# First expert search with masks in halves, bank-held thresholds and a new order of its neighbours

## The chip, the cores and the metric

The kernel runs on one core of a Trainium2 chip. The metric is the device time of one execution in microseconds; the time of a kernel is the median of its runs. The core's engines are TensorE (PE; the loading of its weights is shown apart as PEld), VectorE (DVE), ScalarE (ACT), GpSimd (POOL) and SyncE (SP), each with a queue of its own that it works through in order. Transfers are issued by SP and POOL and carried by 16 DMA engines.

## The reference

A local and summary attention gives 1536 tokens of 512 numbers. They go through a mixture of 8 experts of exactly 192 tokens each, then through a dense layer pair (`_moe2_ref`). What matters here is how tokens come to experts: all 12288 logits are walked from the largest down, and a token goes to an expert that still has room.

```python
def _moe_ref(x, w_gate, w1, w2):
    N, D = x.shape
    E = w_gate.shape[1]
    cap = N // E
    order = np.argsort(-(x @ w_gate).flatten())
    assigned = -np.ones(N, dtype=np.int64)
    counts = np.zeros(E, dtype=np.int64)
    for idx in order:
        tok, e = int(idx) // E, int(idx) % E
        if assigned[tok] >= 0 or counts[e] >= cap:
            continue
        assigned[tok] = e
        counts[e] += 1
    ...
    for e in range(E):
        mask = assigned == e
        out[mask] = np.maximum(x[mask] @ w1[e], 0.0) @ w2[e]
    return out

def _moe2_ref(x, w_in, w_out):
    h = x @ w_in
    g = np.where(h >= 1, h, np.where(h <= -1, 0.0, (h + 1) ** 2 / 4))
    return g @ w_out
```

## The kernel before

**The search.** The greedy walk is done in eight phases, one for each expert that fills up. `Router.phase(k)` (line 554) works on 128 partitions by `NT` = 12 token columns. The token's best open expert is `oh` (one-hot). A threshold is found in `LEVELS` = 5 rounds of `KARY` = 32 steps: VectorE makes a mask `mk` of every token against 32 levels (line 713, in `pairwise`); twelve small matmuls (line 601) count the tokens over each level for each expert; VectorE subtracts the room that is left, reduces, and makes flags `fl`; one matmul (line 611) adds the flags up to the next offset `c`, in PSUM. After the last round the members: `vz` is the distance to the threshold, `cm` compares it with -0.5 and +0.5 of the last step, `X` holds who is assigned. A matmul (line 624) and a reduction `nn` (line 641) count per expert, two matmuls (line 635) and an ACT copy `tot` (line 638) give the totals ahead of every column, `f`, `fm`, `es` choose the expert that is full, `ei` is its number (SP reads it, to address the weights), `pos` and `slot` give every token its place, and `S` is a one-hot of places in two halves (line 713 again). `place` (line 722) multiplies it with `num`, the token numbers; the result, copied by ACT to `idx`, is a list of 192 tokens. The first phase runs alone; each later one runs beside the products of the expert before.

**The experts.** `fetch(k)` (line 759) gathers the 192 rows by POOL in two indirect DMAs of 96 rows; for `k == 0` SP also stores 32 bytes of the second half away, so SP waits there for that half. `weights(k, j)` issues four transfers of 1 MB for expert `k` from SP as soon as its number is known (stage "expert") and a slot is free. `transposed(k, h)` (line 797) turns one half of the tokens with four PE transposes, and ACT copies it to `xt`. `mlp(k)` is 64 steps: 32 first-layer products (line 816) and 32 second-layer ones (line 825). PE handles one such float32 product as two passes, each shown as one instruction of 192 columns; so "x6" of the trace are three products.

**What sets the order.** `run_experts` writes both threads into PE's queue. For each stage the search yields, one number of `PLAN` is taken. For the first `WAIT` stages after the first list was placed, and before that, the number is a count of blank matmuls (line 745, on a tile of zeros); the two stages named in `HALVES` also turn a half of the first expert's tokens. After that the number is a count of products. The tokens of expert `k + 1` are turned in `products()` at step 48 of `mlp(k)`, if they are placed by then. VectorE's conversions for the dense layers are also handed out here, one every `PACE` stages.

Of the kernel before, what the change touches and what calls it, by code (L numbers as in the profile page):

```python
# [8 lines left out]
F32 = mybir.dt.float32  # L9
# [24 lines left out]
RAWS = 9  # L34

PLAN = """
3 2 3 2 1 2 2 2 2 2 2 2 2 2 1 10 12 3 2 2 2 3 3 3 3 3 2 2 9 9 2 3 3 3 3 3 3 3 3 2 2 16 9 3 3 3 3 3 3 3 3 3 2 2 10
12 2 3 3 3 3 3 3 3 3 2 2 10 9 3 4 3 3 4 3 3 3 3 2 2 10 9 2 3 3 3 4 3 3 3 3 2 2 10 6 8 10
"""

WAIT = 5
HALVES = 3, 4

PACE = 4
TAIL = 2
# [368 lines left out]
class Router:  # L414
# [19 lines left out]
    def consts(self):  # L434
# [18 lines left out]
            g.tensor_scalar(self.lev[j], ki[:, :KARY], float(KARY) ** -j, None, op0=OP.mult)  # L453
            g.memset(self.unit[j], float(KARY) ** -j)
        self.rev = st.tile([128, E], BF, name="rev")
        self.num = st.tile([128, E], F32, name="num")
        g.tensor_scalar(self.rev, ki[:, :E], -1.0, E + 1.0, op0=OP.mult, op1=OP.add)
        g.tensor_scalar(self.num, ki[:, :E], -1.0, None, op0=OP.add)
        self.tok = st.tile([128, NT], HF, name="tok")
        t = st.tile([128, NT], F32, name="tokf")  # L460
        g.iota(t, pattern=[[128, NT]], base=0, channel_multiplier=1, allow_small_or_imprecise_dtypes=True)
# [92 lines left out]
    def phase(self, k):  # L554
# [13 lines left out]
        if not last:  # L568
            oh = self.oh
            for j in range(LEVELS):  # L570
# [9 lines left out]
                                                   c[:, :, None].to_broadcast([128, NT, 2]), op0=OP.subtract,  # L580
                                                   op1=OP.subtract)
                mk = wk.tile([128, NT, KARY], BF, name="mk")
                self.pairwise(mk, zi, self.lev[j], OP.is_ge)
                if k and j == 0:
                    self.close()
                if j < LEVELS - 1:
# [21 lines left out]
                nc.vector.tensor_scalar(fl, fm.to_broadcast([KARY, 2]), 0.0, None, op0=OP.is_ge)  # L608
                yield "flags"
                p = self.ps()  # L610
                nc.tensor.matmul(p[:, :2], self.unit[j][:KARY], fl, start=True, stop=True)
                c = p[:, 0:1].to_broadcast([128, NT])
            v = wk.tile([128, NT], F32, name="vz")
            nc.vector.tensor_tensor(v, zi[:, :, 0], c, op=OP.subtract)

            cm = wk.tile([128, 2] + full[1:], BF, name="cm")
            vb = v[:, :, None].to_broadcast(full)
            for i in range(2):
                nc.vector.scalar_tensor_tensor(cm[:, i], vb, (i - 0.5) * u, oh, op0=OP.is_ge, op1=OP.mult)
            nc.vector.tensor_tensor(X[:, 0], self.asg, cm[:, 1], op=OP.add)  # L620
            nc.vector.tensor_tensor(X[:, 1], cm[:, 0], cm[:, 1], op=OP.subtract)
            yield "members"
            pn = self.ps()
            nc.tensor.matmul(pn[:, :2 * NT * E], self.unit[0], cm.rearrange("p i t e -> p (i t e)"),
                             start=True, stop=True)
        else:

            self.close()
            nc.vector.tensor_copy(X[:, 0], self.asg)
            nc.vector.tensor_scalar(X[:, 1], v[:, :, None].to_broadcast(full), 0.0, None, op0=OP.is_ge)  # L630
            yield "members"

        pt = self.ps()
        for i in range(2):
            nc.tensor.matmul(pt[:NT * E, i * 128:(i + 1) * 128], X[:, i].rearrange("p t e -> p (t e)"), self.unit[0],
                             start=(i == 0), stop=(i == 1), skip_group_check=True)
        tot = wk.tile([NT * E, 2, 128], BF, name="tot")
        nc.scalar.activation(tot.rearrange("p i q -> p (i q)"), pt[:NT * E, :256], AF.Copy)
        if not last:
            nn = wk.tile([128, 2, E], F32, name="nn")  # L640
            nc.vector.tensor_reduce(nn, pn[:, :2 * NT * E].rearrange("p (i t e) -> p i e t", i=2, e=E),
                                    axis=AX.X, op=OP.add)
            nc.vector.tensor_tensor(f, nn[:, 0], self.left, op=OP.is_ge)
        else:
            nc.vector.tensor_scalar(f, self.left, CAP + 0.5, None, op0=OP.is_lt)
# [3 lines left out]
                                       op0=OP.mult, op1=OP.max, accum_out=fm)  # L649
        es = wk.tile([128, E], BF, name="es")  # L650
        nc.vector.tensor_scalar(es, f2, fm, None, op0=OP.is_equal)
        en = wk.tile([128, 1], F32, name="en")
        scr = wk.tile([128, E], F32, name="scr2")
        nc.vector.scalar_tensor_tensor(scr, es, 1.0, self.num, op0=OP.mult, op1=OP.mult, accum_out=en)
        ei = self.wk.tile([1, 1], I32, name="ei", bufs=4)
        nc.vector.tensor_copy(ei, en[:1])
        self.expert[k] = ei
        yield "expert"
        XE = wk.tile([128, 2] + full[1:], BF, name="XE")
        nc.vector.tensor_tensor(XE.rearrange("p i t e -> p (i t) e"), X.rearrange("p i t e -> p (i t) e"),  # L660
                                es[:, None, :].to_broadcast([128, 2 * NT, E]), op=OP.mult)
        p = self.ps()
        q = p[:, :2 * NT * E]
        nc.tensor.matmul(q, self.upto, X.rearrange("p i t e -> p (i t e)"), start=True, stop=False)
# [14 lines left out]
        for h in range(2):  # L679
            s = slice(NT // 2 * h, NT // 2 * (h + 1))  # L680
            self.pairwise(S[:, s], lo[:, s], self.slots, OP.is_equal)
            if h == 0:
                num = wk.tile([128, NT, 2], HF, name="num")
                nc.vector.tensor_tensor(num[:, :, 1], self.tok, hi, op=OP.mult)
                nc.vector.tensor_tensor(num[:, :, 0], self.tok, num[:, :, 1], op=OP.subtract)
            yield "half"
        yield "slots"
        self.place(k, S, num)
# [1 line left out]
        if not last:  # L690

            t1 = wk.tile([128, NT], F32, name="t1")
            nc.vector.tensor_scalar(t1, slot, 0.5, None, op0=OP.is_ge)
            nc.vector.scalar_tensor_tensor(t1, slot, CAP + 0.5, t1, op0=OP.is_lt, op1=OP.mult)
            nc.vector.scalar_tensor_tensor(t1, v, 0.5 * u, t1, op0=OP.is_ge, op1=OP.add)
            yield "left"
            nc.vector.scalar_tensor_tensor(Z, t1[:, :, None].to_broadcast(full), -8192.0, Z, op0=OP.mult, op1=OP.add)
            nc.vector.scalar_tensor_tensor(Z, es[:, None, :].to_broadcast(full), -8192.0, Z, op0=OP.mult, op1=OP.add)
            self.books = X, nn, es
# [27 lines left out]
class Experts:  # L727
# [72 lines left out]
    def mlp(self, k):  # L800

        nc = self.nc
        xt = self.XT.pop(k)
        ht = self.wk.tile([128, 8, CAP], F32, name="ht", bufs=1)
        at = 96 * (k - 4) if k >= 4 else 192 * (k % 2)

        def turn(n):
            if self.post and n % 6 == 3:
                self.post.pop(0)()

        n = 0
        for f in range(8):
            w = self.W[k, f // 4]
            p = self.pp.tile([128, CAP], F32, name="acc", bufs=4)
            for c in range(4):
                nc.tensor.matmul(p, w[:, c, f % 4 * 128:f % 4 * 128 + 128], xt[:, c], start=(c == 0), stop=(c == 3))  # L816
                turn(n)
                n += 1
                yield
            nc.scalar.activation(ht[:, f], p, AF.Relu)  # L820
        for c in range(4):
            w = self.W[k, 2 + c // 2]
            p = self.pp.tile([128, CAP], F32, name="acc", bufs=4)
            for f in range(8):
                nc.tensor.matmul(p, w[:, f, c % 2 * 128:c % 2 * 128 + 128], ht[:, f], start=(f == 0), stop=(f == 7))  # L825
                turn(n)
                n += 1
                yield
            o = self.ff.R[:, 0::3] if c < 2 else self.ff.R[:, 1:3]
            nc.scalar.activation(o[:, :, c % 2, at:at + 96], p.rearrange("p (h n) -> p h n", h=2), AF.Copy)  # L830
        if k < 4:
            self.post += self.ff.combine(k, at)
        yield
        yield
# [485 lines left out]
```

## Time and profile before

| | us |
|---|---|
| median of 3 runs (lowest to highest) | 586.96 (586.51 to 587.66) |
| the profiled execution, own time | 586.25 |
| its span in the trace | 584.2 |
| PE busy | 565.4 (97%) |
| DVE busy | 407.1 (70%) |
| ACT busy | 277.2 (47%) |
| POOL busy | 177.7 (30%) |

The span is the time from the first to the last recorded instruction; 2.05 us of the profiled execution lie outside it. PE's busy time counts blank matmuls too. The stages along the span: attention to about 94 us, the first search alone to 115.5 us, experts (with the later searches beside them) to about 316 us, the dense layers to the end. Views of the trace give start and duration of an instruction, its line, its output and input tile and, in brackets, how long its engine had stood idle and what ended that.

### The profile page before, as it was taken

Reading aid. Unit: us, or ns where it says so; the run is one execution under the profiler, and the core shown is the slowest. Engines: PE = TensorE matmul, PEld = TensorE weight load, DVE = VectorE, ACT = ScalarE, POOL = GpSimd, SP = SyncE. Lnnn points to the kernel's source line nnn. Section 1 sums busy time; section 2 is a strip of 40 time slices with the busy share of each in tenths; the row PEclk is TensorE's granted clock in tenths of the full one; section 3 lists DMA queues with packets and bytes.
Section 4 is the critical chain, followed back from the end, with each engine's and each line's share of the span. In section 5 each row is a group of like instructions: output and inputs, shape, how many; then the busy total and the mean of one; then the engine's idle time right before and its main releaser. Section 6 shows DMA issues by size and latency. Waiting matters only on the chain.

```text
span 584.2 us, 11399 instructions
## 1 busy us (share of the span) xinstructions
PE 565.4 (97%) x4284; PEld 483.8 (83%) x4289; DVE 407.1 (70%) x1096; ACT 277.2 (47%) x637; POOL 177.7 (30%) x274
## 2 busy tenths in 40 slices
PE   6899999999999999999999999999999999999996
PEld 3568684487888888999999988889888989898984
DVE  7887776763665756665675899886699986666550
ACT  5576760121312221323223566666577766666653
POOL 5412100110101101114002443333455875555424
PEclk9999999999999999999999999999999999999999
DMA  9999114396729449485886223200000200000002
GB/s 213 197 204 212 39 75 149 107 313 211 259 64 310 177 139 315 156 241 198 270 272 218 72 75 106 73 3 0 1 0 1 91 19 1 1 1 1 2 0 108
DMA packets 84104, 71.43 MB, mean 122 GB/s; under 512 B 42562, under 2 KB 71234, under 8 KB 84050
## 3 DMA queue, kind: packets, MB, share of 16 engines
q1 hardware_dynamic: 81506, 64.38, 38.9%
q0 software_dynamic: 2016, 6.33, 3.3%
q8 instruction: 33, 0.54, 0.4%
q14 instruction: 21, 0.17, 0.1%
q10 hardware_dynamic: 528, 0.02, 0.1%
HBM read 64.41 MB, written 6.30 MB: 121 GB/s over the span
## 4 chain that ended last, share of the span: by engine, by line
PE 69%; DVE 6%; issue 2%; POOL 2%; DMA 1%; ACT 1%; POOLq 0%; DVEq 0%
PE po L1090 18%; PE ph L1057 17%; PE acc L816 15%; PE acc L825 13%; PE rt L601 2%; DMA xg<-xdram,idx 1%; DVE gl L1073 1%; PE px L797 1%; POOL out_dram L1108 1%; PE rt L722 1%; DVE slot L979 1%; PE px L745 1%; DVE u L1068 1%; DVE c L1160 1%; PE px L1057 1%
## 5 line engine op out<-in xcount | busy, mean ns | idle before, releaser
L825 PE MATMUL acc<-ht,slot 128*128 128x192 f32 x512 | 95.3, 333 | 0.0
L816 PE MATMUL acc<-xt,slot 128*128 128x192 f32 x512 | 94.3, 333 | 0.0
L825 PEld LDWEIGHTS acc<-ht,slot 128*128 128x128 f32 x512 | 82.3, 190 | 0.5
L816 PEld LDWEIGHTS acc<-xt,slot 128*128 128x128 f32 x512 | 82.3, 190 | 0.5
L1035 POOL TENSOR_TENSOR al<-sums,ah 128x256 fp32r<-128x256 f32 x64 | 54.2, 849 | 88.1 <-ACT ah L1034 78.6
L1057 PE MATMUL ph<-yh,ah 128*128 128x384 f32 x218 | 75.1, 344 | 1.5 <-DVE c L1160 1.1
L1090 PE MATMUL po<-wl,gh 128*128 128x512 f32 x192 | 75.8, 395 | 0.1
L1090 PE MATMUL po<-wh,gh 128*128 128x512 f32 x192 | 75.8, 395 | 0.0
L1090 PE MATMUL po<-wh,gl 128*128 128x512 f32 x192 | 75.8, 395 | 0.0
L1057 PE MATMUL ph<-yl,ah 128*128 128x384 f32 x218 | 73.7, 338 | 0.0
L1057 PE MATMUL ph<-yh,al 128*128 128x384 f32 x218 | 73.6, 338 | 0.0
L1035 POOL TENSOR_TENSOR al<-slot,ah 128x256 fp32r<-128x256 f32 x48 | 42.6, 888 | 77.4 <-PE ph L1057 41.0
L1070 ACT ACTIVATE gh<-u 128x384 fp32r<-128x384 f32 x64 | 33.4, 522 | 58.7 <-DVE u L1068 58.4
L759 POOL DMA_INDIRECT xg<-xdram,idx x16 | 15.0, 938 | 147.7 <-ACT idx L724 99.0
L1073 DVE TENSOR_TENSOR gl<-u,gh 128x384 fp32r<-128x384 f32 x64 | 50.9, 795 | 6.5 <-ACT gh L1070 6.4
L820 ACT ACTIVATE ht<-acc 128x192 f32<-128x192 f32 x64 | 21.2, 331 | 67.4 <-PE acc L816 66.8
L1057 PEld LDWEIGHTS ph<-yh,ah 128*128 128x128 f32 x218 | 40.9, 188 | 9.8 <-DVE c L1160 3.3
L1057 PEld LDWEIGHTS ph<-yl,ah 128*128 128x128 f32 x218 | 41.0, 188 | 3.9
L1189 DVE TENSOR_TENSOR u<-ph,x 128x384 f32<-128x384 f32 x32 | 17.7, 553 | 34.1 <-PE ph L1057 34.1
L830 ACT ACTIVATE yr<-acc 128x192 f32<-128x192 f32 x32 | 10.6, 330 | 65.0 <-PE acc L825 65.0
L1090 PEld LDWEIGHTS po<-wh,gl 128*128 128x128 f32 x192 | 36.2, 188 | 5.9
L1057 PEld LDWEIGHTS ph<-yh,al 128*128 128x128 f32 x218 | 41.0, 188 | 0.0
(237 smaller groups left out, 1012.8 us busy)
## 6 DMA issues: line engine op xcount, KB each, us to landing
slot<-in_moe_w_dram SPq DMA_DIRECT2D x31, 1024.0 KB, 7.9
raw<-in_moe_w_in_dram SPq DMA_DIRECT2D x16, 512.0 KB, 4.2
raw<-in_moe_w_out_dram SPq DMA_DIRECT2D x16, 512.0 KB, 6.6
vw<-in_v_dram SPq DMA_DIRECT2D x20, 192.0 KB, 5.1
nat<-in_k_dram SPq DMA_DIRECT2D x12, 256.0 KB, 5.6
nat<-in_q_dram SPq DMA_DIRECT2D x12, 256.0 KB, 4.8
xdram<-xs SPq DMA_DIRECT2D x12, 256.0 KB, 2.0
slot<-in_moe_w_dram SPq DMA_DIRECT2D x2, 512.0 KB
```

The lines of the kernel that those rows point to most:

```text
L601: nc.tensor.matmul(p[:KARY, :E], mk[:, t], oh[:, t], start=(t == 0), stop=(t == NT - 1))
L759: nc.gpsimd.indirect_dma_start(out=self.XG[k][:, h], out_offset=None, in_=self.x, in_offset=bass.IndirectOffsetOnAxis(ap=idx[:, h:h + 1], ...
L816: nc.tensor.matmul(p, w[:, c, f % 4 * 128:f % 4 * 128 + 128], xt[:, c], start=(c == 0), stop=(c == 3))
L820: nc.scalar.activation(ht[:, f], p, AF.Relu)
L825: nc.tensor.matmul(p, w[:, f, c % 2 * 128:c % 2 * 128 + 128], ht[:, f], start=(f == 0), stop=(f == 7))
L830: nc.scalar.activation(o[:, :, c % 2, at:at + 96], p.rearrange("p (h n) -> p h n", h=2), AF.Copy)
L1035: nc.gpsimd.tensor_tensor(l, x, h.bitcast(F32), op=OP.subtract)
L1057: nc.tensor.matmul(p, w[:, 128 * c:128 * c + 128], y[:, b, c], start=first and n == 0, stop=n == 5, skip_group_check=True)
L1070: nc.scalar.activation(gh, u, AF.Copy)
L1073: nc.vector.tensor_tensor(gl, u, gh.bitcast(F32), op=OP.subtract)
L1090: nc.tensor.matmul(self.po[t], x[:, c], w, start=(self.left[t] == 6 * self.PAIRS - 1), stop=(self.left[t] == 0))
L1189: nc.vector.tensor_tensor(u2 if j == 1 else u3, p, x1, op=OP.add)
```

## The change

Eight edits, most of them in `phase`:

- For `k == 0` the mask `mk` is made in two instructions of six columns each.
- A matmul of a new constant `edges` (-0.5, +0.5) is added in front of the last flag matmul, into the same PSUM tile. The two columns then hold the offset less and plus half a step, and `cm` compares `zi` with them directly; `vz` comes later. (Line 695 is adapted.)
- The totals (`pt`) go to the upper half of the PSUM tile that the counts (`pn`) use, instead of a tile of their own.
- `nn` is reduced in two instructions, the second behind `XE`.
- The expert's number `ei` is worked out by ACT from `fm`; three VectorE instructions go.
- For `k == 0` the two products `num` are made by POOL.
- `WAIT`, `HALVES` and four entries of `PLAN` (3 2 2 2 become 2 2 3 5): products begin two stages sooner, the first expert's halves are turned one stage sooner.
- The four products of the first output block of the first expert are done for 96 columns, then for the other 96.

```diff
 PLAN = """
-3 2 3 2 1 2 2 2 2 2 2 2 2 2 1 10 12 3 2 2 2 3 3 3 3 3 2 2 9 9 2 3 3 3 3 3 3 3 3 2 2 16 9 3 3 3 3 3 3 3 3 3 2 2 10
+3 2 3 2 1 2 2 2 2 2 2 2 2 2 1 10 12 2 2 3 5 3 3 3 3 3 2 2 9 9 2 3 3 3 3 3 3 3 3 2 2 16 9 3 3 3 3 3 3 3 3 3 2 2 10
...
-WAIT = 5
-HALVES = 3, 4
+WAIT = 3
+HALVES = 2, 3
...
-        self.num = st.tile([128, E], F32, name="num")
...
-        g.tensor_scalar(self.num, ki[:, :E], -1.0, None, op0=OP.add)
+        self.edges = st.tile([1, 2], BF, name="edges")
+        for i in range(2):
+            g.memset(self.edges[:, i:i + 1], i - 0.5)
...
                 mk = wk.tile([128, NT, KARY], BF, name="mk")
-                self.pairwise(mk, zi, self.lev[j], OP.is_ge)
+                for s in (slice(0, NT),) if k else (slice(0, NT // 2), slice(NT // 2, NT)):
+                    self.pairwise(mk[:, s], zi[:, s], self.lev[j], OP.is_ge)
...
                 p = self.ps()
-                nc.tensor.matmul(p[:, :2], self.unit[j][:KARY], fl, start=True, stop=True)
+                if j == LEVELS - 1:
+                    nc.tensor.matmul(p[:, :2], self.unit[j][:1], self.edges, start=True, stop=False)
+                nc.tensor.matmul(p[:, :2], self.unit[j][:KARY], fl, start=(j < LEVELS - 1), stop=True)
                 c = p[:, 0:1].to_broadcast([128, NT])
+
+            cm = wk.tile([128, 2] + full[1:], BF, name="cm")
+            zb = zi[:, :, 0:1].to_broadcast(full)
+            for i in range(2):
+                nc.vector.scalar_tensor_tensor(cm[:, i], zb, p[:, i:i + 1], oh, op0=OP.is_ge, op1=OP.mult)
+            nc.vector.tensor_tensor(X[:, 0], self.asg, cm[:, 1], op=OP.add)
+            nc.vector.tensor_tensor(X[:, 1], cm[:, 0], cm[:, 1], op=OP.subtract)
             v = wk.tile([128, NT], F32, name="vz")
             nc.vector.tensor_tensor(v, zi[:, :, 0], c, op=OP.subtract)
-
-            cm = wk.tile([128, 2] + full[1:], BF, name="cm")
-            vb = v[:, :, None].to_broadcast(full)
-            for i in range(2):
-                nc.vector.scalar_tensor_tensor(cm[:, i], vb, (i - 0.5) * u, oh, op0=OP.is_ge, op1=OP.mult)
-            nc.vector.tensor_tensor(X[:, 0], self.asg, cm[:, 1], op=OP.add)
-            nc.vector.tensor_tensor(X[:, 1], cm[:, 0], cm[:, 1], op=OP.subtract)
...
             nc.tensor.matmul(pn[:, :2 * NT * E], self.unit[0], cm.rearrange("p i t e -> p (i t e)"),
-                             start=True, stop=True)
+                             start=True, stop=False, skip_group_check=True)
...
-        pt = self.ps()
+            pn = self.ps()
+
+        pt = pn[:, 256:]
         for i in range(2):
             nc.tensor.matmul(pt[:NT * E, i * 128:(i + 1) * 128], X[:, i].rearrange("p t e -> p (t e)"), self.unit[0],
-                             start=(i == 0), stop=(i == 1), skip_group_check=True)
+                             start=(last and i == 0), stop=(i == 1), skip_group_check=True)
...
-            nc.vector.tensor_reduce(nn, pn[:, :2 * NT * E].rearrange("p (i t e) -> p i e t", i=2, e=E),
-                                    axis=AX.X, op=OP.add)
+            ne = pn[:, :2 * NT * E].rearrange("p (i t e) -> p i e t", i=2, e=E)
+            nc.vector.tensor_reduce(nn[:, 0], ne[:, 0], axis=AX.X, op=OP.add)
...
-        en = wk.tile([128, 1], F32, name="en")
-        scr = wk.tile([128, E], F32, name="scr2")
-        nc.vector.scalar_tensor_tensor(scr, es, 1.0, self.num, op0=OP.mult, op1=OP.mult, accum_out=en)
         ei = self.wk.tile([1, 1], I32, name="ei", bufs=4)
-        nc.vector.tensor_copy(ei, en[:1])
+        nc.scalar.activation(ei, fm[:1], AF.Copy, bias=float(E), scale=-1.0)
...
                                 es[:, None, :].to_broadcast([128, 2 * NT, E]), op=OP.mult)
+        if not last:
+            nc.vector.tensor_reduce(nn[:, 1], ne[:, 1], axis=AX.X, op=OP.add)
...
                 num = wk.tile([128, NT, 2], HF, name="num")
-                nc.vector.tensor_tensor(num[:, :, 1], self.tok, hi, op=OP.mult)
-                nc.vector.tensor_tensor(num[:, :, 0], self.tok, num[:, :, 1], op=OP.subtract)
+                e = nc.vector if k else nc.gpsimd
+                e.tensor_tensor(num[:, :, 1], self.tok, hi, op=OP.mult)
+                e.tensor_tensor(num[:, :, 0], self.tok, num[:, :, 1], op=OP.subtract)
...
-            nc.vector.scalar_tensor_tensor(t1, v, 0.5 * u, t1, op0=OP.is_ge, op1=OP.add)
+            nc.vector.scalar_tensor_tensor(t1, v, u, t1, op0=OP.is_ge, op1=OP.add)
...
-            for c in range(4):
-                nc.tensor.matmul(p, w[:, c, f % 4 * 128:f % 4 * 128 + 128], xt[:, c], start=(c == 0), stop=(c == 3))
+            halves = (slice(0, 96), slice(96, 192)) if k == f == 0 else (slice(0, CAP),)
+            for i in range(4 * len(halves)):
+                c, s = i % 4, halves[i // 4]
+                nc.tensor.matmul(p[:, s], w[:, c, f % 4 * 128:f % 4 * 128 + 128], xt[:, c, s], start=(c == 0), stop=(c == 3))
+                if (i + 1) % len(halves):
+                    continue
                 turn(n)
```

On PE, where the first expert's products begin (`xg` are the gathered tokens, `unit` serves the flag matmuls, `slot_1688` and `slot_1689` are the first weights), stands before:

```order
L797 MATMUL px<-ident,xg 128x96 x4
L611 LDWEIGHTS unit_508
L611 MATMUL rt<-fl,unit_508 128x2
...
L601 MATMUL rt<-oh,mk 32x8
L816 MATMUL acc<-xt,slot_1688 128x192 x3
L611 LDWEIGHTS unit_509
L611 MATMUL rt<-fl,unit_509 128x2
```

and now:

```order
L802 MATMUL px<-ident,xg 128x96 x4
...
L603 MATMUL rt<-oh,mk 32x8
L823 MATMUL acc<-xt,slot_1689 128x96 x6
L615 LDWEIGHTS unit_508
L615 MATMUL rt<-fl,unit_508 128x2
L823 MATMUL acc<-xt,slot_1689 128x96 x2
L823 MATMUL acc<-xt,slot_1689 128x192 x4
```

The products stand one flag step (`unit_508` instead of `unit_509`) and one mask step sooner in the second phase; with the new counts 36 instead of 28 stand ahead of that phase's line 722.

On PE, from the second phase's placing matmuls to the turning of the second expert's tokens, before:

```order
L722 MATMUL rt<-num,S 96x2
L816 MATMUL acc<-xt,slot_1689 128x192 x4
L825 MATMUL acc<-ht,slot_1690 128x192 x5
...
L825 MATMUL acc<-ht,slot_1690 128x192 x2
...
L825 MATMUL acc<-ht,slot_1690 128x192 x3
...
L825 MATMUL acc<-ht,slot_1691 128x192
L797 MATMUL px<-ident,xg 128x96 x8
L825 MATMUL acc<-ht,slot_1691 128x192 x2
```

and now:

```order
L727 MATMUL rt<-num,S 96x2
L834 MATMUL acc<-ht,slot_1691 128x192 x9
...
L834 MATMUL acc<-ht,slot_1691 128x192 x2
L615 LDWEIGHTS unit_507
L615 MATMUL rt<-fl,unit_507 128x2
L834 MATMUL acc<-ht,slot_1691 128x192
L834 MATMUL acc<-ht,slot_1692 128x192
L802 MATMUL px<-ident,xg 128x96 x8
```

Between the two stand 13 products, one mask step and one flag step, where there were 21 products, three mask steps and two flag steps.

On VectorE, at the end of the first phase (with the semaphores that each instruction waits for), before:

```order
L641 TENSOR_REDUCE nn<-rt 128x16 [waits DMAHW7_49,PE_49]
L643 TENSOR_TENSOR f<-nn,left 128x8 [waits DVE_49]
...
L651 TENSOR_SCALAR es<-f_1942,fm_1941 128x8 [waits DVE_49]
L654 SCALAR_TENSOR_TENSOR scr_1947,en<-es,num 128x8 [waits DVE_49]
L656 CAST ei<-en 1x1 [waits DVE_49]
L660 TENSOR_TENSOR XE<-X,es 128x192
L668 TENSOR_TENSOR pos<-rt,XE 128x192 [waits DMAHW4_49,DVE_49,PE_49]
```

and now:

```order
L625 TENSOR_TENSOR vz<-zi,rt 128x12 [waits DMAHW7_49]
L647 TENSOR_REDUCE nn<-rt 128x8 [waits Activation_49]
...
L656 TENSOR_SCALAR es<-f_1948,fm_1947 128x8 [waits DVE_49]
L662 TENSOR_TENSOR XE<-X,es 128x192 [waits DVE_49]
L665 TENSOR_REDUCE nn<-rt 128x8
L672 TENSOR_TENSOR pos<-rt,XE 128x192 [waits DMAHW4_49,DVE_49,PE_49]
```

`nn` waited for PE and waits for ACT now; the expert's number is gone from the row, and the second half of `nn` stands between `XE` and `pos`.

## Rows read from the trace of the kernel before

**Rows 1.** Stretch: us, PE PEld DVE ACT POOL busy (x), PEclk, DMA share, GB/s

```profile
153.00:560.00 407.00, 405.24 (x2432) 367.48 (x2432) 291.75 (x695) 199.78 (x460) 139.77 (x156) 1.00 0.33 107
```

**Rows 2.** Timelines (start us, us long) of PE, POOL, SP where products begin.

```profile
115.53 0.76 PE L816 MATMUL acc<-xt,slot 128*128 128x192 f32 x3
...
110.08 0.92 POOL L759 DMA_INDIRECT xg<-xdram,idx  x1 [0.30 <-issue]
...
113.17 0.31 SPq L763 DMA_DIRECT2D spare<-xg  x1
```

**Rows 3.** PE timeline and, last, chain: second expert's placing, gather, turning.

```profile
127.63 0.66 PE L722 MATMUL rt<-num,S 128*96 128x2 f16 x12
...
138.47 0.55 PE L797 MATMUL px<-ident,xg 96*128 96x96 f32 x4 [0.56 <-DMA xg<-xdram,idx]
...
129.99 8.44 DMA xg<-xdram,idx
```

**Rows 4.** DVE and ACT timelines, first search; last a POOL group (us, mean ns).

```profile
96.08 0.36 DVE L713 TENSOR_TENSOR mk<-zi,lev 128x384 bf16<-128x384 bf16 x1
...
102.91 0.17 DVE L614 TENSOR_TENSOR vz<-zi,rt 128x12 f32<-128x12 bf16 x1 [0.29 <-PE rt L611]
103.11 0.43 DVE L619 SCALAR_TENSOR_TENSOR cm<-vz,oh 128x96 bf16<-128x96 f32 x2
...
103.89 0.35 DVE L641 TENSOR_REDUCE nn<-rt 128x16 f32<-128x192 f32 x1
...
104.95 0.17 DVE L654 SCALAR_TENSOR_TENSOR scr<-es,num 128x8 f32<-128x8 bf16 x1
...
105.23 0.24 DVE L660 TENSOR_TENSOR XE<-X,es 128x192 bf16<-128x192 bf16 x1
105.56 0.36 DVE L668 TENSOR_TENSOR pos<-rt,XE 128x192 f32<-128x192 f32 x1
...
106.77 0.46 DVE L713 TENSOR_TENSOR S<-lo,slots 128x576 f16<-128x576 bf16 x1
107.14 0.17 DVE L684 TENSOR_TENSOR num<-tok,hi 128x12 f16<-128x12 f16 x1
...
107.43 0.45 DVE L713 TENSOR_TENSOR S<-lo,slots 128x576 f16<-128x576 bf16 x1
...
104.32 0.38 ACT L638 ACTIVATE tot<-rt 96x256 bf16<-96x256 f32 x1 [13.81 <-PE rt L635]
...
L458 POOL TENSOR_SCALAR num<-ki 128x8 f32<-128x8 f32 x1 | 0.3, 251 | 0.1
```

**Rows 5.** Chain that ended last: start us, us, what, second phase.

```profile
110.98 0.39 PE rt L601 x12
...
116.77 0.11 PE rt L611
116.88 1.17 PE acc L816 x6
...
123.52 0.36 PE rt L635 x2
...
127.79 0.51 PE rt L722 x12
...
147.68 5.23 PE acc L816 x32
```

**Rows 6.** DMA of 128.7 to 132.9 us (queue, packets, MB, share); gathers under weights.

```profile
q1 hardware_dynamic: 835, 1.68, 104.9%
...
DMA to landing us min/median/max: 6.1/7.4/8.4
```

**Rows 7.** PE timelines with blanks (start, two stretches); last the stretch 580 to 584.

```profile
1.93 3.90 PE L373 MATMUL ptr<-warm 128*128 128x512 bf16 x9 [1.93 <-DVE warm L371]
...
108.23 2.10 PE L745 MATMUL px<-blank 128*128 128x512 bf16 x9
...
580.00:584.00 4.00, 0.00 (x0) 0.00 (x0) 0.00 (x0) 0.00 (x0) 0.41 (x1) 0.80 0.23 88
```

## The prediction

> **What bounds the kernel now.** I read the stretches first. From 153 to 560 us TensorE is busy 405.24 of 407.00 us, and of the expert stage before that it lacks little; VectorE is busy 291.75 us and waits for TensorE most of the rest [rows 1]. So the program ends when TensorE has done its fixed work, and the change can be worth two things only: the time at which real products begin (115.53 us, line 816 [rows 2]), and what TensorE waits or idles after that. Until then TensorE turns blank matmuls and the first search runs as a chain of short VectorE instructions. Then I read what the start waits for: the gather of the first 192 tokens is issued in halves, the second at 110.08 us, and SyncE's small store behind it, which waits for that half, starts at 113.17 us [rows 2]. Last I read the gather for the second expert: issued at 129.99 us, landed 8.44 us later, and the turning of its second half is the one place after the start where TensorE visibly waits, 0.56 us, at 138.47 us [rows 3]. I shall call the placing matmuls of the second phase (line 722, first at 127.63 us) P, and the turning of the second expert's tokens (line 797) T.
>
> **The change part by part: the first search.** Masks in halves. An instruction on 384 columns takes 0.36 us, one on 576 takes 0.46 us [rows 4]; the slope puts 192 columns at 0.26 us. TensorE can start 0.10 us sooner, and its first six matmuls (half of 0.39 us for twelve [rows 5]) end at 0.45 us, when the second half, started about 0.17 us after the first, has just ended (0.43 us). Five levels: -0.50 us. Bounds: -0.5 and, if TensorE waits for the whole mask, five times 0.07, +0.35 us. I take -0.50: the row of 576 columns and its follower 0.37 us later show how instructions overlap. Thresholds: `cm` starts where `vz` started, 102.91 instead of 103.11 us [rows 4], -0.20 us.
>
> Counts and totals now share a bank, and the order shows what comes of it: the reduction `nn` waits for ScalarE, that is, for `tot`. `nn` began at 103.89 us; `tot` runs from 104.32 for 0.38 us, to 104.70 [rows 4]. Both sooner by 0.70 us (0.50 and 0.20), `tot` ends at 104.00 and `nn` starts at 104.05. From `nn` to `pos` it was 1.67 us; the expert number taken from VectorE saves 0.28 (104.95 to 105.23), the halved `nn` about 0.10 (it loses half its 0.35 us above a floor), the other half, now ahead of `pos`, costs up to 0.15 and some 0.10 of that is waiting between dependent instructions that goes too: 1.25 us. `pos` starts at 105.30 instead of 105.56: -0.26 us where the shorter chain alone would give a full -1 us. The two small `num` products leave VectorE: 107.43 becomes 107.14, -0.29 us; on GpSimd a tiny operation took 0.25 us [rows 4], so two are done by 106.8, before the first half of `S` ends (106.97). Sum at the index list: **-0.55 us**. The expert number from ScalarE comes about 0.35 us sooner, but its first weights move while the search still runs and nobody waits for them: 0.
>
> **The start of the products.** The gather's landing moves with the list, from 113.13 us, just ahead of SyncE's store, to 112.58. Two turns are taken out between landing and products, so now the turning of the first expert's second half waits for the landing: at 112.65, 0.40 us; then twelve mask matmuls, 0.39 us; first product at **113.45 us** instead of 115.53, -2.08 us. The products by halves cost nothing much: a 192-column pass takes 0.163 us (5.23 us for 32 [rows 5]); two 96-column passes I bound by 0.16 and, if weight loads do not hide, 0.25 us; eight passes, 0 to +0.7 us, and I take 0.
>
> **The second phase.** Here the order decides. Thirty-six products now stand before P instead of twenty-eight, thirteen instead of twenty-one between P and T. P moves: a product is two passes, 0.327 us, eight more are 2.62 us; one mask and one flag step that stood before the products now stand among them, and each break costs 0.19 us besides its own 0.39 or 0.11 (six passes take 1.17 us between breaks, 0.98 in a run [rows 5]), 0.58 and 0.30 us. P comes at 113.45 + (127.63 - 115.53) + 2.62 + 0.88 = 129.05. It may also wait for `S`: eleven products (3.6 us) and the 0.25 us of the prefix matmuls stand between the totals' matmuls (end 123.88 [rows 5]) and P, 3.85 us; on VectorE, with `nn` behind `tot` by 0.04 + 0.38 + 0.05 us, the 3.99 us from `nn` to the end of `S` (103.89 to 107.88), less 0.38 for what is taken out, make 4.1 us. +0.2 us, and the same in later phases, where more products stand there, is hidden. P: **129.3 us**, later than the 127.63 of before, although the products began 2.1 us sooner. The gather of the second expert follows P, so it cannot land sooner either. TensorE however arrives at T sooner after P: 0.51 + 13 x 0.327 + 0.58 + 0.30 = 5.64 us (the same sum for before gives 0.51 + 21 x 0.327 + 3 x 0.58 + 2 x 0.30 = 9.72; measured 9.7: the second half's 138.47 less its wait of 0.56 and as much again as its own 0.55 for the first half, 137.36, less 127.63 [rows 3]), at 134.9. The gather was issued 2.36 us behind P's start (129.99 against 127.63) and lands at P + 2.36 + 8.44 us = **140.1 us** [rows 3]. TensorE, which works in order, waits about 4.8 us at T (5.2 less the turning of the first half), in two pieces, where it waited 0.56. Why the gather is slow is in the trace: it is issued while 4 MB of weights for the same expert are under way, and from 128.7 to 132.9 us, with it issued, 835 packets of the weights moved and none of the gather's [rows 6]. The weights' issue moves with the second phase just as P does, so nothing in the change parts the two.
>
> **Sum.** T's second half: 140.1 against 138.47, +1.65 us, with equally many products done. But before, two mask steps and one flag step of the third phase lay behind TensorE by then; now they lie ahead: 2 x 0.58 + 0.30 = +1.46 us. The edges' extra matmul in five more phases (about 0.1 each) is paid by the sooner `cm`: 0. The other way round: -2.08 + 0.88 + 0.2 + (4.8 - 0.56) = +3.2. At T for the third expert 24 products remain after its placing: 0.51 + 7.85 + 3 x 0.58 + 2 x 0.30 = 10.7 us, against 2.36 + 7.4 for the median gather [rows 6]: covered by 0.9 us; for the slowest (8.44) not quite, 0.1 us. Later ones have more room. Behind, TensorE is full, and what is late stays late: **+3.1 us**. The profiled execution, 586.25 us (span 584.2 and 2.05 around it), would be 589.4; the median of the runs shown lies 0.71 above it, so 586.96 becomes **590.1 us**. A measurement of this kernel can tell some 0.2%, 1.2 us, from no change.
>
> **Rivals.** First, *the clock falls in the wait*. The gap is 4.8 us with the first half's transposes somewhere in it. For it: nine blank matmuls at the very start, behind an idle TensorE, took 3.90 us, and the same nine just before the products 2.10 us. Against it: over the last four microseconds, with no matmul in them, the granted clock still averages 0.80 [rows 7]. If it falls, one stretch like that start costs 3.90 - 2.10 = 1.8 us more: 591.9 us.
>
> Second, *the gather gets its share*. The Trainium skill (DMA: Bandwidth & Descriptors, Queues, rings and completion order) says each DMA engine "round-robins between the queue rows it has work for"; by that rule the gather would not stand behind the weights, and the time would be about 586.9 us. The rows disagree for this gather (no packet in 4.2 us). Worked out from rows: alone, the first gather's second half landed 3.05 us after issue (110.08 to 113.13); of that at most 2.13 follow the issuing instruction (0.92 us long [rows 2]), and with half of the engines' time they would take as much again, 5.2 us: T at 129.3 + 2.36 + 5.2 = 136.9, -1.6 + 1.46 = -0.1 us, 586.9. The quickest of the gathers under weights, 6.1 us [rows 6], gives 137.8, +0.8 us, 587.8. This is the case of no change.
>
> Third, on the other side, *the gather is there in time*: landed as fast as alone, 3.05 us after issue, before TensorE arrives at 134.9. Then T's second half begins at 135.3: -3.2 + 1.46 = -1.7 us, **585.3 us**. It decides from a landing 4.1 us after issue downward, T's second half at 135.8. For it: the first expert's weights end earlier. Against it: no gather of the seven that run beside weights landed under 6.1 us.
>
> Fourth, *the search is not shortened* (TensorE waits for whole masks): the start moves 0.5 to 0.9 us back and everything with it, 590.6 to 591.0; part of the forecast's spread.
>
> **How the numbers follow.** Forecast, the fourth with it, 0.56; clock 0.08; shared queue 0.18; in time 0.18. The predicted time is the first's, 590.1. Its own range, with the halves' bound and gathers of 7.4 to 9 us, is 588.7 to 591.4; the range given takes in the clock (591.9) and the shared queue (586.9, with 0.4 us for the search below it), and leaves out the third: 586.6 to 592.0. Faster by over 0.2%: 0.18; within: 0.18; slower: 0.64.
>
> **What would show it.** Right: the first product near 113.4 us, P near 129 us, a wait of 3 to 5 us at T ended by the gather, and the same distance from there on. `nn` behind `tot` in the DVE rows; `S` halves 0.37 us apart. Wrong: a gather that lands within 4.1 us of its issue, or a P that is no later than before; then the sooner start is kept. A granted clock of half after T would be the first rival.

## The result: slower by 1.2%

The changed kernel takes 593.92 us (median of 4 runs, 592.12 to 594.81), the kernel before 586.74 us in the same comparison: a ratio of 1.0116 (95% interval 1.009 to 1.0142). The direction was forecast, the size was not: +7.2 us where +3.1 was expected, and 593.9 lies above the range (586.6 to 592.0). The profiled execution of the changed kernel took 594.81 us, with a span of 593.0 us.

The two profiled executions do not begin the search at the same time. This is the input of the first mask in the kernel before, in the changed one, and in an experiment below (new order) whose program up to that point is the one of before (DVE timelines: start us, us, engine, line, what):

```profile
94.03 0.18 DVE L576 TENSOR_SCALAR zi<-v 128x24 bf16<-128x24 f32 x1
```

```profile
95.53 0.18 DVE L577 TENSOR_SCALAR zi<-v 128x24 bf16<-128x24 f32 x1
```

```profile
95.38 0.18 DVE L576 TENSOR_SCALAR zi<-v 128x24 bf16<-128x24 f32 x1
```

So the 1.5 us ahead of the search are not the change. From here on all positions count from that instruction and are called z + so many us; the span then ends at z + 490.17 before and z + 497.47 now, +7.3 us; the medians differ by 7.2.

PE's timeline of the changed kernel around T, the turning of the second expert's tokens (the numbers in brackets are idle time and what ended it):

```profile
115.39 1.58 PE L823 MATMUL acc<-xt,slot 128*128 128x96 f32 x12
...
131.45 0.79 PE L727 MATMUL rt<-num,S 128*96 128x2 f16 x12
...
140.17 0.88 PE L802 MATMUL px<-ident,xg 96*128 96x96 f32 x4 [2.71 <-DMA xg<-xdram,idx]
142.23 0.90 PE L802 MATMUL px<-ident,xg 96*128 96x96 f32 x4 [1.18 <-DMA xg<-xdram,idx]
...
146.50 2.29 PE L834 MATMUL acc<-ht,slot 128*128 128x192 f32 x6
148.72 0.48 PE L603 MATMUL rt<-oh,mk 128*32 128x8 bf16 x12
149.13 1.88 PE L834 MATMUL acc<-ht,slot 128*128 128x192 f32 x6
150.95 0.17 PE L615 MATMUL rt<-fl,unit 32*128 32x2 bf16 x1
151.05 1.24 PE L834 MATMUL acc<-ht,slot 128*128 128x192 f32 x6
```

Products begin at z + 19.86 (z + 21.50 before), P (the second phase's placing matmuls) at z + 35.92 (33.60), and the second half of T at z + 46.70 (44.44): TensorE has waited 2.71 and 1.18 us for the gather, where it waited 0.56 [rows 3]. Behind each wait the four transposes of a half take 0.88 and 0.90 us, where the second half took 0.55 before [rows 3], and six passes take 2.29 us, until they take 1.24 again at 151.05. The stretches say why (us, then PE, PEld, DVE, ACT and POOL busy, granted clock, DMA share, GB/s), changed kernel first, before second:

```profile
140.00:150.00 10.00, 8.65 (x50) 7.00 (x51) 1.43 (x10) 1.31 (x3) 0.00 (x0) 0.51 0.57 168
```

```profile
140.00:150.00 10.00, 9.76 (x76) 8.01 (x76) 5.78 (x33) 1.37 (x4) 0.00 (x0) 1.00 0.11 33
```

The granted clock averages 0.51 over these ten microseconds, the lower of its two levels (1.2 of 2.4 GHz), though PE is busy again from 142.2 us. Two more stretches of the changed kernel place the fall:

```profile
137.50:140.20 2.70, 0.03 (x1) 0.03 (x1) 0.01 (x1) 0.01 (x1) 0.00 (x0) 1.00 1.09 266
140.40:150.40 10.00, 8.82 (x51) 7.16 (x51) 1.43 (x10) 1.31 (x3) 0.00 (x0) 0.50 0.52 157
```

The clock was still granted in full while TensorE stood idle; it fell as the transposes began and was at half for some ten microseconds. What has to be priced are these two things: a wait, and after it slow products.

### The profile page after: what moved, and what is told of

Its sections match the earlier page's. It is cut to its first block, busy times and chain, and to the rows that moved or that the text cites. A ratio compares the mean times of both kernels' runs of the same rounds, so it can differ in the third digit from the quotient of the medians.

```text
span 593.0 us, 11418 instructions
## 1 busy us (share of the span) xinstructions
PE 570.8 (96%) x4299; PEld 488.1 (82%) x4299; DVE 406.2 (69%) x1082; ACT 278.3 (47%) x645; POOL 178.3 (30%) x277
## 4 chain that ended last, share of the span: by engine, by line
PE 74%; DVE 11%; issue 6%; DMA 3%; ACT 2%; POOL 2%; POOLq 0%; SPq 0%; DVEq 0%; ACTq 0%
PE po L1099 18%; PE ph L1066 17%; PE acc L823 13%; PE acc L834 11%; PE rt L603 2%; PE po L319 2%; PE ps L281 1%; PE pt L305 1%; DMA xg<-xdram,idx 1%; DMA nat<-in_k_dram 1%; PE ptr L213 1%; DVE gl L1082 1%; PE px L750 1%; PE ptr L352 1%; POOL out_dram L1117 1%
## 5 line engine op out<-in xcount | busy, mean ns | idle before, releaser
L834 PE MATMUL acc<-ht,slot 128*128 128x192 f32 x512 | 98.4, 340 | 0.0
L823 PE MATMUL acc<-xt,slot 128*128 128x192 f32 (+1 forms) x520 | 94.9, 332 | 0.0
L834 PEld LDWEIGHTS acc<-ht,slot 128*128 128x128 f32 x512 | 84.9, 195 | 0.5
L1099 PEld LDWEIGHTS po<-wl,gh 128*128 128x128 f32 x192 | 36.1, 188 | 5.6 <-POOL wl L1057 0.4
```

Source lines behind the costliest of these rows:

```text
L823: nc.tensor.matmul(p[:, s], w[:, c, f % 4 * 128:f % 4 * 128 + 128], xt[:, c, s], start=(c == 0), stop=(c == 3))
L1099: nc.tensor.matmul(self.po[t], x[:, c], w, start=(self.left[t] == 6 * self.PAIRS - 1), stop=(self.left[t] == 0))
```

## Experiments

All positions below are read from the same timelines: the members' comparison `cm`, the counts' reduction `nn`, the first half of the one-hot `S`, the second issue of the first gather, the first product, P, the second half of T (where both halves stand in one row, its start), the end of the span. Each row is read from one trace. The kernels with the search as changed, the shared bank included, have `cm` between 8.51 and 8.65 and the gather between 15.83 and 15.97, so a tenth of a microsecond between two rows says little. The last column has the median of the runs and, in brackets, that of the kernel before, run beside it; where there was one run, only its trace is used.

| kernel | cm | nn | S | gather | product | P | T | end | median us (before beside it) |
|---|---|---|---|---|---|---|---|---|---|
| before | 9.08 | 9.86 | 12.74 | 16.05 | 21.50 | 33.60 | 44.44 | 490.17 | 586.74 |
| changed | 8.52 | 10.27 | 12.80 | 15.84 | 19.86 | 35.92 | 46.70 | 497.47 | 593.92 (586.74) |
| new order alone | 9.08 | 9.86 | 12.73 | 16.05 | 20.40 | 35.99 | 45.49 | 494.82 | 592.21 (587.10) |
| changed, old order | 8.51 | 10.26 | 12.79 | 15.83 | 21.30 | 33.88 | 44.62 | 490.78 | 587.71 (587.10) |
| blanks in both waits | 8.65 | 10.41 | 12.93 | 15.97 | 20.06 | 36.13 | 46.94 | 494.17 | 591.19 (587.10) |
| blanks in the first wait | 8.53 | 10.28 | 12.80 | 15.84 | 19.90 | 35.96 | 46.79 | 494.02 | 590.43 (586.64) |
| T late | 8.52 | 10.27 | 12.79 | 15.83 | 19.89 | 35.94 | 47.46 | 489.27 | 586.52 (587.10) |
| gather first | 8.51 | 10.26 | 12.79 | 15.83 | 19.89 | 36.30 | 42.15 | 489.66 | 586.68 (587.03) |
| T late, own banks | 8.53 | 9.51 | 12.13 | 15.17 | 19.22 | 35.37 | 46.75 | 488.30 | 585.23, one run |
| T late, full width | 8.57 | 10.32 | 12.84 | 15.88 | 20.18 | 35.79 | 47.30 | 489.10 | 586.43, one run |
| both of these | 8.51 | 9.50 | 12.11 | 15.15 | 19.49 | 35.17 | 46.56 | 488.01 | 584.94 (587.03) |
| own banks, masks whole | 8.93 | 9.92 | 12.53 | 15.58 | 19.65 | 35.81 | 47.20 | 488.69 | 585.38, one run |
| own banks, `num` on VectorE | 8.52 | 9.50 | 12.13 | 15.44 | 19.52 | 35.71 | 47.10 | 488.61 | 585.75, one run |

### Is it the order?

The new order alone, put into the kernel before:

```diff
-3 2 3 2 1 2 2 2 2 2 2 2 2 2 1 10 12 3 2 2 2 3 3 ...
+3 2 3 2 1 2 2 2 2 2 2 2 2 2 1 10 12 2 2 3 5 3 3 ...
-WAIT = 5
-HALVES = 3, 4
+WAIT = 3
+HALVES = 2, 3
```

> The kernel before with PLAN, WAIT and HALVES of the changed one, and nothing else. Theory (the order makes the loss): a wait of 3 to 5 us at T, a granted clock below 0.9 in the stretch 115 to 153 us, 593 to 595 us. Rival (the edits of the search make it): products begin 1.6 us sooner and nothing is lost, 585.1 us.

And the reverse of that diff in the changed kernel:

> The changed kernel with PLAN, WAIT and HALVES of before; every edit of the search and the products by halves stay. Theory (the loss comes from the order alone: TensorE comes to T, the turning of the second expert's tokens, before their gather has landed, and its clock falls in the wait): T waits no more than half a microsecond, the granted clock stays at full, 586.7 less 0.2 us for the shorter search plus up to 0.8 us for the products in halves, 586.3 to 587.3 us. Rival (the edits of the search cost the time, the shared bank above all): it stays within a microsecond of the changed kernel, 593 to 595 us.

The new order alone costs 0.89% (ratio 1.0089, 1.007 to 1.0108), the edits with the old order nothing that can be told (1.0007, 0.9997 to 1.0016; the trace has 0.6 us more, inside the 0.8 that was allowed for the halves; the 587.71 us are 0.4 above the stated range, and the kernel before beside them is 0.4 above its 586.74 too). New order alone at T, and its stretch:

```profile
139.95 0.55 PE L797 MATMUL px<-ident,xg 96*128 96x96 f32 x4 [2.70 <-DMA xg<-xdram,idx]
140.87 0.90 PE L797 MATMUL px<-ident,xg 96*128 96x96 f32 x4 [0.36 <-DMA xg<-xdram,idx]
```

```profile
140.00:150.00 10.00, 9.63 (x60) 7.83 (x60) 2.22 (x14) 1.31 (x3) 0.00 (x0) 0.66 0.49 153
```

The rival, that the edits of the search lose the time, falls. The 592.21 us are 0.8 below the lower end of what was expected for the new order: the second half of its gather landed 1.2 us sooner than the changed kernel's, counted from z, and the lower clock did not last as long (six passes take 1.24 us again at 147.76). Why it landed sooner and why the lower clock ended sooner is open. The rows above show besides that the first four transposes behind the wait of 2.70 us still ran at full speed (0.55 us); only the next four were slow.

### The wait and the clock apart

```diff
                 if n == 48 and placed[0] > k + 1:
-                    turn(k + 1)
+                    for h, m in ((0, 12), (1, 6)):
+                        if k == 0:
+                            ex.idle(m)
+                        turn(k + 1, (h,))
```

> The changed kernel with blank matmuls (twelve before the first half of T, six before the second), as long as TensorE's wait there. If the fall of the clock costs what the trace of the changed kernel says (3.6 us of products at the lower level and half a microsecond of slow transposes): the gather lands as late as before, TensorE is never idle there, the granted clock stays at full, and the time is 593.9 less 4.0, 589.9 us (589.2 to 590.6). If the loss is all wait and the clock costs nothing: 593.9 us, the same.

In a second version the blanks stand before the first half only (`if k == 0 and h == 0`):

> The changed kernel with twelve blank matmuls before the first half of T and none before the second, so that only the second wait (1.2 to 1.5 us) is left idle. If the clock fell in the first, long wait: it stays at full here and the time is that of the kernel with blanks in both, 591.2 us. If a wait of a little over a microsecond is enough: slow transposes and products behind the second half, 592.5 to 594 us.

The second version, at T and in the stretch:

```profile
136.82 2.32 PE L750 MATMUL px<-blank 128*128 128x512 bf16 x10
139.24 0.55 PE L802 MATMUL px<-ident,xg 96*128 96x96 f32 x4
141.37 0.52 PE L802 MATMUL px<-ident,xg 96*128 96x96 f32 x4 [1.58 <-DMA xg<-xdram,idx]
141.73 0.52 PE L834 MATMUL acc<-ht,slot 128*128 128x192 f32 x2
```

```profile
140.00:150.00 10.00, 8.63 (x77) 7.00 (x77) 3.08 (x19) 1.47 (x4) 0.00 (x0) 1.00 0.49 147
```

T's second half starts at z + 46.79, as late as without blanks (46.70), so the gather lands when it did; but the clock is granted in full and the end comes 3.45 us sooner (494.02 against 497.47; the medians, each less that of the kernel before beside it, say 3.4). That is the price of the clock. Behind an idle wait of 1.58 us, standing alone, it did not fall; behind the one of 2.71 us (2.70 with the new order alone) it did. What is left, 494.02 - 490.17 = 3.85 us, is the price of the wait and of what stands ahead of it. The forecast had +3.1 for that. The kernel T late, below, has no wait and ends at z + 489.27: the wait is worth 494.02 - 489.27 = 4.75 us, and without it the change is 0.90 us ahead of before. Blanks in both waits came out at 591.19 us, above the expected 589.2 to 590.6: the end moved by 3.3 us (497.47 to 494.17), not by 4.0. The second rival of that run, that the clock costs nothing, falls in both.

### What takes the wait away

T later by twelve products for the second expert:

```diff
-                if n == 48 and placed[0] > k + 1:
+                if n == (60 if k == 0 else 48) and placed[0] > k + 1:
```

> The changed kernel with T twelve products later for the second expert (step 60 of the first expert's 64 instead of 48), 25 products between P (the second phase's placing matmuls) and T. Theory: TensorE comes to T some 11.3 us after P and the gather lands 10.7 us after it, so it does not wait, the clock stays, and the sooner start is kept: P stood 1.2 us ahead of before when counted in equal work, so 585.5 less the 0.56 us that before waits at T, 585.0 us, with 0.5 us to either side. Rival (the search's edits): the wait goes but 3 to 4 us remain lost, 588 to 590 us.

And the gather ahead of the weights, with T where it was:

```diff
-        if k == 0:
+        if k <= 1:
             nc.sync.dma_start(self.spare, self.XG[k][:1, 1, :8])
...
-                if r == "expert":
+                if r == "expert" and k != 1:
                     known[0] = k + 1
                 if r == "places":
                     ex.fetch(k)
+                    known[0] = k + 1
```

> The changed kernel, with the second expert's weights held back: SyncE makes its small store behind the second expert's gather too, and asks for its 4 MB of weights only after that. T stays at step 48. If the weights that are under way make the gather late: it lands some 3 to 3.5 us after its second issue as the first expert's does, before TensorE is at T (5.6 us after P, 3.1 us after the issue), T waits under 0.7 us, the clock stays, and the time is 7.3 us less than the changed kernel's less what the weights' own lateness costs (first megabyte wanted some 14 us after P): near the kernel with T later, 586 to 587 us. If the gather is slow by itself: it lands 7 to 8 us after its issue as before and T waits, 591 to 594 us.

Both bring the time back to that of before: 586.52 us (ratio 0.9995, 0.9986 to 1.0005) and 586.68 us (0.9993, 0.9983 to 1.0003). T late was expected to gain 1.7 us (585.0, half a microsecond to either side), and missed that; the trace has 0.9 (490.17 to 489.27), and the next group tells where the rest went. In the second, PE comes to T as early as in the changed kernel and finds the tokens there. POOL's second issue, SP's store that waits for that half, and PE:

```profile
134.53 0.92 POOL L764 DMA_INDIRECT xg<-xdram,idx  x1 [0.30 <-issue]
```

```profile
137.65 0.25 SPq L768 DMA_DIRECT2D spare<-xg  x1
```

```profile
137.14 0.92 PE L834 MATMUL acc<-ht,slot 128*128 128x192 f32 x4
137.89 0.83 PE L802 MATMUL px<-ident,xg 96*128 96x96 f32 x8
```

The gather lands 3.1 us after its issue, and T shows no wait. With the weights under way it took 8.2 us in the changed kernel (issue at 133.94, T at 142.23), and this is what the DMA engines did from that issue for 3.6 us, from 133.9 to 137.5 (queue, packets, MB, share; q1 carries the weights, q0 the gathers):

```profile
q1 hardware_dynamic: 709, 1.31, 96.9%
q0 software_dynamic: 23, 0.09, 7.4%
```

The same two queues in gather first, 134.5 to 137.7 us, print one row, without weights:

```profile
q0 software_dynamic: 128, 0.39, 44.5%
```

So the weights that are under way make the gather late; that is shown, not only argued. The changed kernel's rows from the first half's issue to 137.0 us, and from there to 141.5 us, show in what way:

```profile
q1 hardware_dynamic: 847, 1.69, 102.9%
```

```profile
q1 hardware_dynamic: 831, 0.86, 76.0%
q0 software_dynamic: 128, 0.39, 32.4%
```

For 4.3 us the gather does not move at all; then all of its 128 packets pass beside the weights. In gather first it begins to move within 1.5 us of its first issue (133.31 us; 29 packets from 134.8 to 135.5). Why it stands still is not shown. By the Trainium skill (DMA: Bandwidth & Descriptors, Queues, rings and completion order) each DMA engine takes turns between the queues that it has work for; by that the gather would not stand still while the weights move. The trace disagrees up to 137.0 us, with no packet of the gather against 847, and is in line with it from there on.

### What the edits of the search are worth

These stand on T late, which has no wait at T. Totals in a bank of their own and one reduction of the counts, as before the change:

```diff
...
-        pt = pn[:, 256:]
+        pt = self.ps()
...
-            nc.vector.tensor_reduce(nn[:, 0], ne[:, 0], axis=AX.X, op=OP.add)
+            nc.vector.tensor_reduce(nn, ne, axis=AX.X, op=OP.add)
...
-        if not last:
-            nc.vector.tensor_reduce(nn[:, 1], ne[:, 1], axis=AX.X, op=OP.add)
```

> The changed kernel with T at step 60, totals in a bank of their own again and the counts' reduction in one piece, as before the change. Measured from the first mask's input to the second issue of the first gather. If the shared bank is what ate the search's gain: the counts' reduction starts some 0.95 us sooner (it need not wait for the copy of the totals) and the issue comes 0.8 us sooner than in the changed kernel, 15.0 us instead of 15.84, and the first product with it. If not: 15.8 us.

The end of `cm`'s chain in the changed kernel, and with the banks apart:

```profile
104.96 0.16 DVE L625 TENSOR_TENSOR vz<-zi,rt 128x12 f32<-128x12 bf16 x1
105.80 0.26 DVE L647 TENSOR_REDUCE nn<-rt 128x8 f32<-128x96 f32 x1 [0.69 <-ACT tot L643]
```

```profile
104.63 0.16 DVE L625 TENSOR_TENSOR vz<-zi,rt 128x12 f32<-128x12 bf16 x1
104.71 0.35 DVE L645 TENSOR_REDUCE nn<-rt 128x16 f32<-128x192 f32 x1
```

VectorE stood idle for 0.69 us until the copy of the totals was done, and does not any more; `nn` starts 0.76 us sooner (0.95 was expected), the gather is issued 0.66 us sooner (z + 15.17; 15.0 was expected), the end comes 0.97 us sooner. More than half of that is the start; the rest comes later. Placing matmuls of the third and of the eighth list, T late and then with its own banks:

```profile
155.04 0.66 PE L727 MATMUL rt<-num,S 128*96 128x2 f16 x12
...
255.38 0.66 PE L727 MATMUL rt<-num,S 128*96 128x2 f16 x12
```

```profile
154.44 0.66 PE L723 MATMUL rt<-num,S 128*96 128x2 f16 x12
...
254.27 0.66 PE L723 MATMUL rt<-num,S 128*96 128x2 f16 x12
```

The distance grows from 0.60 to 1.11 us: the shared bank and the reduction in two pieces, which were undone together, cost some 0.1 us in each later phase too, which the prediction had at nothing. At full width, against both of these, the same distance grows by the same 0.51 us. What each of the two edits costs there was not run. By the Trainium skill (PSUM — Partial Sum Buffer, PSUM bank collisions raise a hardware error) PSUM has to be guarded with semaphores by bank, "not by address". The trace is in line with that: `nn` waits for a copy of columns that it does not read.

The first products at full width, as if `halves` were always `(slice(0, CAP),)`:

> The changed kernel with T at step 60 and the first output block in passes of 192 columns. If the halves cost: from the first product to P 0.5 us less than the 16.05 us with halves, and the first product where it was (19.9 us after the first mask's input). If the halves hide something: P no sooner.

From the first product to P 15.61 us instead of 16.05, so the halves cost 0.44 us; but the first product starts at z + 20.18 instead of z + 19.89. PE's row there names the cover that the halves give, the copy of the second half's tokens:

```profile
115.68 1.24 PE L823 MATMUL acc<-xt,slot 128*128 128x192 f32 x6 [0.19 <-ACT xt L803]
```

Net, the halves cost 0.15 to 0.2 us. Both together:

> Both of these together with T at step 60. If the two costs are separate they add up: 0.8 and 0.5 us less than the kernel that only has T later (0.6 us under before), 585.2 us, 0.3% under the kernel before. If P waits for something else by then: no better than 586.2 us.

584.94 us against 587.03, ratio 0.9968 (0.9955 to 0.998): faster than both kernels. The two gains add up within a tenth or so: 0.97 and 0.17 us at the end singly, 1.26 together. Two edits undone singly on top of the own banks:

```diff
-                for s in (slice(0, NT),) if k else (slice(0, NT // 2), slice(NT // 2, NT)):
+                for s in (slice(0, NT),):
```

> The kernel with T at step 60 and banks of their own, with the first search's masks in one piece again. Measured from the first mask's input to the members' comparison. If the halves brought most of the gain there: 9.0 us instead of 8.53, and the second issue of the first gather 0.5 us later, 15.65 us. If the thresholds from PSUM brought it: 8.6 us.

```diff
-                e = nc.vector if k else nc.gpsimd
+                e = nc.vector
```

> The kernel with T at step 60 and banks of their own, with the first search's two products of token numbers back on VectorE. If GpSimd brings what was forecast: the second half of the one-hot of places starts 0.29 us later and the second issue of the first gather comes at 15.45 us instead of 15.17. If the placing matmuls waited for GpSimd instead: 15.2 us, no later.

Whole masks cost 0.40 us at `cm` (8.93 against 8.53); the 0.15 us left of the change's 0.56 (9.08 to 8.93) are the thresholds. `num` on VectorE issues the gather 0.27 us later.

## Why the prediction was wrong in size

- **What bounds the kernel.** Right: TensorE's order and its waits decided, and the end moved by what happened at T.
- **The search.** Forecast -0.55 us at the list, measured -0.21 at the gather's issue (16.05 to 15.84). Masks brought 0.40, not 0.50; thresholds 0.15, not 0.20; `num` 0.27, as forecast (0.29). That `nn` would come behind `tot` was right, but its place was put at z + 10.02 and is z + 10.27: `cm` starts 0.14 us later than forecast, and on its two new operands takes 0.56 us and not 0.43 [rows 4]. From `nn` to `pos` 1.25 us was forecast and 1.32 measured; the terms given for it (1.67 less 0.28, less 0.10, plus 0.15, less 0.10) add up to 1.34, so this part was a slip in the sum.
- **The start of the products.** Forecast -2.08, measured -1.64: 0.34 us of the gap is the list's.
- **The halves.** Taken at 0 of a bound of 0 to +0.7; 0.44 us measured, less 0.3 for a start that does not wait for the second half's copy, which the prediction did not price.
- **P.** Forecast z + 35.27 (129.3), measured z + 35.92: 0.44 from the start and 0.44 from the halves, less the 0.2 for a wait ahead of P. That wait came inside: P's weight loads stand idle for 0.18 us until VectorE has made `num`, between the halves of `S`, and P takes 0.79 us instead of 0.66 [rows 3], and 0.66 when the banks are apart. That the same wait is hidden in later phases does not fit the 0.1 us that each of them gains with the banks apart.
- **The gather and the wait.** Landing 8.44 us after issue forecast, 8.24 measured; T at z + 46.07 forecast, z + 46.70 measured. Counted from P the second half's transposes start after 10.78 us, where 10.80 was forecast. The wait was put at 4.8 us and came as 3.9 of idle time: TensorE came to T 6.01 us behind P and not 5.64, and the first half's transposes took 0.88 us and not 0.4. Up to here the mechanism is right and the sum short by what P was late: with the clock held up the end is 3.85 us later, forecast +3.1, and nearly all of the difference already stands at T (z + 46.79); from there on it is +1.50 us, and +1.46 was forecast.
- **The clock: the step that failed.** It was the first rival, at a chance of 0.08 and a price of 1.8 us. Against it stood one row, the last four microseconds, where the clock averages 0.80 without a matmul [rows 7]. That row is a mean over a stretch in which the clock fell, as its last two microseconds show by themselves:

```profile
582.00:583.00 1.00, 0.00 (x0) 0.00 (x0) 0.00 (x0) 0.00 (x0) 0.00 (x0) 0.72 0.00 0
583.00:584.00 1.00, 0.00 (x0) 0.00 (x0) 0.00 (x0) 0.00 (x0) 0.00 (x0) 0.50 0.00 0
```

The last matmul had ended at 578.5 us and by 583 us the clock stood at half, so the row did not show a wait of 4.8 us to be safe, but it was read that way. And the price came from a row at the start that lasted 3.90 us [rows 7]; the granted clock of 2 to 6 us reads 1.00 there, so that this row does not show the price of the lower level. Here the products went on slowly from 142.9 to about 150.4 us, and that cost 3.45 us. The range ended at this rival's 591.9 and so had no room for a price twice as large.
- **The other rivals.** The shared queue and the gather in time did not come about. That gather first finds its tokens 3.1 us after the issue shows that the third rival's number was right for a gather alone; here the gather was not alone.

## What to carry to other kernels

When a hand-written order moves real work ahead, list what that work will wait for next: here each product moved ahead of the second list moved its gather back and TensorE's need of it forward. A wait of TensorE is not priced by its length alone: 2.7 idle microseconds cost another 3.45 in slow products. Blank matmuls in the wait saved the 3.45; a later use, or the small transfer ahead of the large one, saved the wait as well. Two results in one PSUM bank put their readers on different engines one behind the other in this program: `cm` came 0.56 us sooner, and `nn` behind it 0.41 us later.

## What was not expected of the hardware

- The granted clock stayed at half for some 8 us of renewed work (142.2 to 150.4 us), twice as long as the slow blanks at the kernel's start [rows 7].
- A gather of 96 rows that lands 3.1 us after its issue alone took 8.2 us beside 4 MB of weights. It did not share with them from the start: no packet of it moved for the first 3.1 us.
- `cm` on `zi` and a threshold from PSUM takes 0.56 us for the pair; on `vz` and a constant it took 0.43 [rows 4]. Which of the two new operands costs it was not run.
